# Moving the w_q checks out of the paired u products, moving the last difference checks, and giving the last two v tiles' products two PSUM banks

## The chip, the cores and the metric

The kernel runs on one core of a Trainium2 chip. The metric is the device time of one execution in microseconds (us). Before the change three runs gave 1128.66, 1130.21 and 1132.23 us; the median is 1130.21 us.

## The reference, cut to what matters

For x of shape 2048 x 512 the result is `x + A(xn) + B(xn)`, with `xn` the layer norm of x. A is a Fourier mixing layer: the real part of a DFT along the sequence of a DFT along the hidden axis, with the four DFT matrices given as inputs. B is a product-key expert layer:

```
q  = xn @ w_q                        # 32 heads, two halves of 128
s1, s2 = q1 @ k1.T, q2 @ k2.T        # 64 scores each
top 2 of s1 x top 2 of s2 -> the best 2 of 4 experts per head, softmax g
act = gelu(xn . u[expert])           # u, v: 4096 x 512
out = sum over 32 heads and 2 experts of g * act * v[expert]
```

Nothing is gathered. The kernel multiplies each tile of 128 tokens by all 4096 rows of u, applies gelu, multiplies the result by a sparse matrix of gates, and multiplies that by all of v.

## The kernel before, in words

The first 430 us load the DFT matrices, compute A, and find the experts of every token (`scores`, `routing`). The change touches only what follows, the last 700 us, where 16 tiles of 128 tokens go through u and v.

**Phases.** The order is z0, z1, v0, then for b = 2, 4, ..., 14 a phase z(b, b+1) that multiplies two tiles at once by u, followed by v(b-1) and v(b), and at last v15. A pair's z phase takes about 41 us (z(14,15) from 1011.1 to 1052.2) and a v phase about 24 us. A z phase of a pair (`z_pair`) is made of slots of 24 matmuls (`slot`, L1173) and of plain groups (`u_part`, L1095). After each slot ScalarE or VectorE takes sums out of the PSUM bank (L1213 to L1227) and ScalarE applies gelu (L1203). A v phase (`v_part`, L1328) runs 16 groups of six 128x512 matmuls into one bank `pv`, two groups for each of its eight steps `cg`; `finish` (L1345) scales the bank onto `y` and stores it. Nine of the sixteen groups of v stay in SBUF. The other seven are loaded again for each tile into three places, by `v_load` (L1306), each when the group before it in that place has been read.

**The gates.** For every tile, four times: `g_mm` builds two one-hot factors L and R on VectorE (L1260, L1265, L1268) and multiplies them on TensorE (L1270); `w_part` multiplies that by the gelu output on VectorE (L1278), rounds it to fp16 on ScalarE (L1285) and forms the remainder on VectorE (L1286). A v phase cannot start before the last `w_part` of its tile.

**The checks.** The kernel relies on structure in its inputs and checks it beside the main work. There are three kinds of check units, each handed out one at a time by `step`:

- `U`, 68 units: `compare` (64) and `compare_w` (4, units 64 to 67) load a block of a DFT matrix, form differences on VectorE (L1359 to L1403, L1426 to L1447) and sum their magnitudes on ScalarE (L1404, L1449). These are the difference checks.
- `F[0]`, 35 units of `fit`: 28 load a block of w_q (L1455) and take the sum of magnitudes on ScalarE (L1456); seven do so with streamed parts of v (L1462, L1463).
- `F[1]`, 25 units: the same on u and v blocks that lie in SBUF (L1467), without a load.

The loads of `U` and `F[0]`, and the product tile of `w_part`, share one pool of four buffers, tag `w`. `step` also holds back the ScalarE part of a unit: it issues those of earlier units, all but the newest. `verdict` gathers all sums into flags, after `step(None)` has flushed the rest at step 3 of v15.

**The order.** The dictionary `plan` says behind which step of which phase a unit or a gate step stands. That is a priority and not a place: the framework orders each engine's instructions itself when the program is built, by its own estimate of when operands and buffers are ready. So a load whose unit stands in the middle of a z phase can be issued near its beginning. Each engine then runs its list in order. All loads and stores of these phases are in SyncE's list.

**The last tile.** In v15 the last two groups (n = 14 and 15, 24 matmuls) are done in two halves of 256 columns, both added into the one bank `pv`. After each half VectorE scales that half onto `y` (L1319), and the half is stored (L1320).

Of the kernel before, what the change touches and what calls it, by code (L numbers as in the profile page):

```python
# [15 lines left out]
ALU = mybir.AluOpType  # L16
# [20 lines left out]
def tile_fnet_peer(ctx, tc, x, ca, cb, c5, wt, wf, wr, wq, kt, ut, vn, out):  # L37
# [9 lines left out]
    nc = tc.nc  # L47
# [503 lines left out]
    w16 = ones.bitcast(F16)  # L551
# [169 lines left out]
    def part_b(safe, stS, stP, stQ, stE, xt, u_sb, cmp_p, w4):  # L721
# [586 lines left out]
        def v_part(b, pv, cg):  # L1308
            w16 = parts(b)
            if b + 1 == NT and cg == 7 and not safe:  # L1310
                for h in range(2):
                    d = slice(h * 256, h * 256 + 256)
                    for n, cc in ((14, 0), (14, 1), (15, 0), (15, 1)):
                        g = v_order(b)[n]
                        for k, (l, r) in enumerate(((0, 0), (0, 1), (1, 0))):
                            nc.tensor.matmul(pv[:, d], w16[:, 2 * g + cc, :, l], v_sb[g][:, r, cc, d], start=False,
                                             stop=(n + cc == 16 and k == 2), skip_group_check=True)
                    y = Y[b]
                    nc.vector.scalar_tensor_tensor(y[:, d], pv[:, d], osc, y[:, d], op0=ALU.mult, op1=ALU.add)  # L1319
                    nc.sync.dma_start(out[b * P:(b + 1) * P, d], y[:, d])  # L1320
                return
            end = 13 if b + 1 == NT and not safe else 15
            for n in (2 * cg, 2 * cg + 1):
                g = v_order(b)[n]
                for cc in range(2):
                    c = 2 * g + cc
                    for k, (l, r) in enumerate(((0, 0), (0, 1), (1, 0))):
                        nc.tensor.matmul(pv, w16[:, c, :, l], v_sb[g][:, r, cc, :], start=(n + cc == 0 and k == 0),  # L1328
                                         stop=(n == end and cc == 1 and k == 2))

                if g >= V2 and g not in [v for v in v_order(b) if v >= V2][-3:]:
                    v_load(PL[g])
# [196 lines left out]
        def take(name):  # L1529
            tag = banks.pop(0)  # L1530
            return psz.tile([P, 512], F32, tag=tag, name=name), tag
# [14 lines left out]
        def put(ph, cg, *fs):  # L1546
            plan.setdefault((ph, cg), []).extend(fs)
# [45 lines left out]
            put(("v", b), 3, lambda b=b: compact_d(b + 2))  # L1593
        put(("z", 14, 15), 8, lambda: compact_d(15))
        if not safe:
            for cg in (1, 3, 5, 7):
                put(("v", 0), cg, F[0])
            for ph, cg in ((("v", 12), 0), (("v", 14), 1), (("v", 14), 3), (("v", 14), 7)):
                put(ph, cg, F[0])
            for ph in phases[3:]:  # L1600
                if ph[0] == "z":
                    put(ph, 8, F[0])
                    for cg in {2: (9, 11, 13, 15), 4: (9, 11, 13, 15), 14: (9, 12)}.get(ph[1], (9, 12, 15)):
                        put(ph, cg, U)
                elif ph[1] < 14:
                    for cg, f in enumerate((None, F[1], F[1], U, U, U, U, F[0]) if ph[1] % 2 == 0 else (
                            None, F[1], F[0], None, U, U, U, F[0])):
                        if f and (ph[1] < 13 or f != U or cg == 6):
                            put(ph, cg, f)
            for cg in range(3):  # L1610
                put(("v", 14), cg, F[1])
                put(("v", 14), cg + 4, U)
                put(("v", 15), cg, F[1])
            for f, n in ((U, 68), (F[0], NK + 16 - V2), (F[1], 16 + V2)):
                assert sum(v.count(f) for v in plan.values()) >= n
# [189 lines left out]
```

## Time and profile before

| what | value |
|---|---|
| median of the runs | 1130.21 us |
| the profiled execution's own time | 1130.3 us |
| its span in the profile | 1128.0 us |
| so outside the span | 2.3 us |
| granted TensorE clock, mean | 0.999 |
| matmuls | 11024 |

The profile's first part gives the busy time of each engine: PE is TensorE's matmuls, PEld its weight loads, DVE VectorE, ACT ScalarE, POOL GpSimd, SP SyncE. A row of the timeline has the start and the length in us, the engine, the line, the operation, the tile written and read, how many are merged, and, in brackets, how long the engine had been idle and what ended that. A row of the waits view names the waiting engine and line, what released it, the total in us, the number of times and the longest. A small q behind an engine's name stands for its sequencer, so SPq rows are issues of transfers.

### The profile page before, as it was taken

Reading aid. Unit: us, or ns where it says so; the run is one execution under the profiler, and the core shown is the slowest. Engines: PE = TensorE matmul, PEld = TensorE weight load, DVE = VectorE, ACT = ScalarE, POOL = GpSimd, SP = SyncE. Lnnn points to the kernel's source line nnn. Section 1 sums busy time; section 2 is a strip of 40 time slices with the busy share of each in tenths; the row PEclk is TensorE's granted clock in tenths of the full one; section 3 lists DMA queues with packets and bytes.
Section 4 is the critical chain, followed back from the end, with each engine's and each line's share of the span. In section 5 each row is a group of like instructions: output and inputs, shape, how many; then the busy total and the mean of one; then the engine's idle time right before and its main releaser. Section 6 shows DMA issues by size and latency. Waiting matters only on the chain.

```text
span 1128.0 us, 28019 instructions
## 1 busy us (share of the span) xinstructions
PE 1109.6 (98%) x11024; PEld 720.0 (64%) x11024; DVE 965.1 (86%) x2883; ACT 667.7 (59%) x1118; POOL 328.6 (29%) x364
## 2 busy tenths in 40 slices
PE   9999999999999999999999999999999999999997
PEld 6455554544545459678479479579469569559643
DVE  7899989989889899885997996997997897887892
ACT  6557698798898465365546545535545635545442
POOL 1415998888889750000000010010010010000000
PEclk9999999999999999999999999999999999999999
DMA  9984456346353215663754854753745755655353
GB/s 285 286 209 164 162 182 202 116 156 200 97 182 111 97 52 187 214 218 118 265 205 153 255 209 141 259 203 146 272 165 189 236 192 197 225 197 188 105 186 107
DMA packets 123932, 206.80 MB, mean 183 GB/s; under 512 B 34564, under 2 KB 65419, under 8 KB 123790
## 3 DMA queue, kind: packets, MB, share of 16 engines
q1 hardware_dynamic: 123488, 204.84, 54.7%
q8 instruction: 88, 1.44, 0.5%
q14 instruction: 54, 0.44, 0.1%
q10 hardware_dynamic: 302, 0.08, 0.0%
HBM read 171.52 MB, written 27.59 MB: 177 GB/s over the span
## 4 chain that ended last, share of the span: by engine, by line
PE 46%; DVE 12%; DMA 3%; ACT 3%; POOL 2%; issue 1%; SPq 0%; ACTq 0%; DVEq 0%; POOLq 0%
PE v L1328 18%; PE z L1173 16%; PE z L1095 9%; PE g L1270 3%; DVE L L1260 2%; DVE w L1278 2%; DMA cx<-in_cb_dram 2%; DVE vals L956 1%; DVE act L1286 1%; DVE idx L960 1%; DMA fit<-in_wq_dram 1%; DVE w L1286 1%; DVE cx L1378 1%; DVE R L1265 1%; DMA v<-v_d 1%
## 5 line engine op out<-in xcount | busy, mean ns | idle before, releaser
L252 PE MATMUL s<-m,xq 128*128 128x512 f16 x1344 | 297.4, 379 | 1.0 <-ACT ss L952 0.5
L1328 PE MATMUL v<-v,act 128*128 128x512 f16 x1044 | 230.8, 379 | 0.3 <-DMA v<-v_d 0.3
L252 PEld LDWEIGHTS <-xq 128*128 128x128 f16 x1344 | 129.8, 98 | 152.2 <-issue 2.5
L1341 POOL TENSOR_TENSOR y<-y,xr 128x512 f32<-128x512 f32 x15 | 28.7, 1915 | 637.9 <-DMA y<-y_d 455.8
L1260 DVE TENSOR_TENSOR L<-io_lam,cmp 128x2048 f16<-128x2048 f16 x128 | 156.1, 1220 | 26.0 <-PE g L1270 25.9
L1328 PEld LDWEIGHTS <-act 128*128 128x128 f16 x1044 | 100.1, 98 | 116.5 <-issue 0.6
L956 DVE MAX8 vals<-ss 128x8 f32<-128x64 f32 x896 | 133.5, 216 | 3.9 <-ACT ss L952 3.9
L1095 PE MATMUL z<-xb,u 128*128 128x128 f16 (+1 forms) x1440 | 121.8, 244 | 0.1
L1173 PEld LDWEIGHTS <-u 128*128 128x128 f16 x2016 | 114.7, 98 | 3.1 <-issue 2.6
L1095 PEld LDWEIGHTS <-u 128*128 128x128 f16 x1440 | 107.6, 98 | 7.5 <-issue 0.2
L1328 PE MATMUL v<-v,w 128*128 128x512 f16 x480 | 106.3, 379 | 0.3 <-DMA v<-v_d 0.3
L952 ACT ACTIVATE ss<-s,wsc 128x512 f32<-128x512 f32 x120 | 81.4, 683 | 38.6 <-PE s L252 33.4
L1404 ACT ACTIVATE cx<-cx 128x896 f32<-128x896 f32 x64 | 60.5, 946 | 67.7 <-DVE cx L1384 38.1
L960 DVE FIND_INDEX8 idx<-vals,ss 128x8 uint16<-128x256 f32 x224 | 93.8, 419 | 0.0
L1173 PEld LDWEIGHTS <-s 128*128 128x128 f16 x1440 | 82.5, 98 | 0.2
L1328 PEld LDWEIGHTS <-w 128*128 128x128 f16 x480 | 46.0, 98 | 53.8 <-issue 0.6
L1285 ACT ACTIVATE act<-w 128x1024 f16<-128x1024 f32 x36 | 48.3, 1358 | 53.8 <-DVE w L1278 49.4
L1270 PEld LDWEIGHTS <-L 128*128 128x128 f16 x2048 | 60.5, 96 | 15.6 <-DVE R L1268 4.2
L1270 PE MATMUL g<-R,L 128*128 128x32 f16 x2048 | 62.0, 176 | 4.3 <-DVE R L1268 4.2
L1278 DVE SCALAR_TENSOR_TENSOR w<-act,scl,g 128x1024 f32<-128x1024 f32 x44 | 55.8, 1277 | 10.3 <-ACT act L1203 10.3
L1173 PE MATMUL z<-xb,u 128*128 128x128 f16 x1008 | 63.1, 219 | 0.4 <-ACT act L1102 0.3
L1173 PE MATMUL z<-x,u 128*128 128x128 f16 x1008 | 61.3, 219 | 1.6 <-ACT w L1226 0.8
(366 smaller groups left out, 1860.8 us busy)
## 6 DMA issues: line engine op xcount, KB each, us to landing
v<-v_d SPq DMA_DIRECT2D x67, 512.0 KB, 4.6
cx<-in_cb_dram SPq DMA_DIRECT2D x64, 448.0 KB, 6.1
s<-s_d SPq DMA_DIRECT2D x42, 512.0 KB, 3.1
w<-in_wq_dram SPq DMA_DIRECT2D x28, 512.0 KB, 6.3
fit<-in_wq_dram SPq DMA_DIRECT2D x28, 512.0 KB, 4.7
uv<-in_vn_dram SPq DMA_DIRECT2D x16, 512.0 KB, 3.8
uv<-in_ut_dram SPq DMA_DIRECT2D x16, 512.0 KB, 4.0
s_d<-v SPq DMA_DIRECT2D x24, 256.0 KB, 4.1
```

The source lines that it names most:

```text
L252: nc.tensor.matmul(ps, xt[i][:, l, kd, :], m[:, r, kd, :], start=(n == 0), stop=(n == 3 * KD - 1))
L952: nc.scalar.activation(s, ps, AF.Copy, scale=inv)
L956: nc.vector.max(vals[:, i, w, :, h], s[:, g, :])
L960: nc.vector.max_index(idx[:, i, w].rearrange("p k h -> p (k h)"), vals[:, i, w, 0:2].rearrange("p k h -> p (k h)"), s[:, w * HC:g + 1, :]. ...
L1095: nc.tensor.matmul(ps if n == 1 else ps.rearrange("p (b n) -> p b n", b=2), ug[:, l, c % 2, kd, :], xb2[:, k0, r, kd, :] if n == 1 else xb ...
L1173: nc.tensor.matmul(bank[:, t * P:(t + 1) * P], lt, rt, start=(t == k == 0 and op in "125"), stop=(t == 3 and k == 5), skip_group_check=op ...
L1260: nc.vector.tensor_tensor(L.rearrange("p t (l two) -> p t l two", two=2), io_lam.rearrange("p (l two) -> p l two", two=2).unsqueeze(1).to_ ...
L1270: nc.tensor.matmul(p[:, hf, t * NC:(t + 1) * NC], L[:, t, :], R[:, t, :], start=True, stop=True)
L1278: nc.vector.scalar_tensor_tensor(w, act[:, :, ts], fw, p.rearrange("p h (n c) -> p c (h n)", c=NC), op0=ALU.mult, op1=ALU.mult)
L1285: nc.scalar.activation(w16[..., 0], w, AF.Copy)
L1328: nc.tensor.matmul(pv, w16[:, c, :, l], v_sb[g][:, r, cc, :], start=(n + cc == 0 and k == 0), stop=(n == end and cc == 1 and k == 2))
L1404: later.append(lambda: nc.scalar.activation(tf[:, P:], tf[:, P:], AF.Abs, accum_out=chk[:, n:n + 1]))
```

## The change

Three things are changed, all for the path that is taken when the inputs are as expected.

1. `F[0]`: the unit behind step 8 of each pair's z phase is removed (seven units). Step 3 of v1, v3, ..., v13 gets one. In v0 the four units behind steps 1, 3, 5, 7 become two behind steps 2 and 6, and step 0 of v2 and of v4 gets one. The total stays 35, and the order of the units stays.
2. `U`: z(6,7) gets a fourth unit, as z(2,3) and z(4,5) have. v13 loses the one behind its step 6. The three behind steps 4, 5 and 6 of v14 go behind steps 6 and 7 of v14 and step 0 of v15. In v14's step 6 the unit stands behind the last `w_part` of tile 15. The total stays 68; since the units are handed out in order, unit 64 moves from v13 to z(14,15), units 65 and 66 to v14's steps 6 and 7, and unit 67 to v15.
3. The last tile: `pv` is complete after group 13 and is scaled onto the whole of `y`. The products of groups 14 and 15 then start new sums, each half in a bank of its own, taken from the four banks that the z and v phases share; each half is then added to `y` and stored.

```
 def v_part(b, pv, cg):
     w16 = parts(b)
     if b + 1 == NT and cg == 7 and not safe:
+        y = Y[b]
+        nc.vector.scalar_tensor_tensor(y, pv, osc, y, op0=ALU.mult, op1=ALU.add)
         for h in range(2):
             d = slice(h * 256, h * 256 + 256)
+            ph = take(f"v{b}_{h}")[0][:, 0:256]
             for n, cc in ((14, 0), (14, 1), (15, 0), (15, 1)):
                 g = v_order(b)[n]
                 for k, (l, r) in enumerate(((0, 0), (0, 1), (1, 0))):
-                    nc.tensor.matmul(pv[:, d], w16[:, 2 * g + cc, :, l], v_sb[g][:, r, cc, d], start=False,
-                                     stop=(n + cc == 16 and k == 2), skip_group_check=True)
-            y = Y[b]
-            nc.vector.scalar_tensor_tensor(y[:, d], pv[:, d], osc, y[:, d], op0=ALU.mult, op1=ALU.add)
+                    nc.tensor.matmul(ph, w16[:, 2 * g + cc, :, l], v_sb[g][:, r, cc, d],
+                                     start=(n + cc == 14 and k == 0), stop=(n + cc == 16 and k == 2))
+            nc.vector.scalar_tensor_tensor(y[:, d], ph, osc, y[:, d], op0=ALU.mult, op1=ALU.add)
             nc.sync.dma_start(out[b * P:(b + 1) * P, d], y[:, d])
         return
...
-            for cg in (1, 3, 5, 7):
-                put(("v", 0), cg, F[0])
+            for ph, cg in ((("v", 0), 2), (("v", 0), 6), (("v", 2), 0), (("v", 4), 0)):
+                put(ph, cg, F[0])
             for ph, cg in ((("v", 12), 0), (("v", 14), 1), (("v", 14), 3), (("v", 14), 7)):
                 put(ph, cg, F[0])
             for ph in phases[3:]:
                 if ph[0] == "z":
-                    put(ph, 8, F[0])
-                    for cg in {2: (9, 11, 13, 15), 4: (9, 11, 13, 15), 14: (9, 12)}.get(ph[1], (9, 12, 15)):
+                    for cg in {2: (9, 11, 13, 15), 4: (9, 11, 13, 15), 6: (9, 11, 13, 15), 14: (9, 12)}.get(ph[1], (9, 12, 15)):
                         put(ph, cg, U)
                 elif ph[1] < 14:
                     for cg, f in enumerate((None, F[1], F[1], U, U, U, U, F[0]) if ph[1] % 2 == 0 else (
-                            None, F[1], F[0], None, U, U, U, F[0])):
-                        if f and (ph[1] < 13 or f != U or cg == 6):
+                            None, F[1], F[0], F[0], U, U, U, F[0])):
+                        if f and (ph[1] < 13 or f != U):
                             put(ph, cg, f)
             for cg in range(3):
                 put(("v", 14), cg, F[1])
-                put(("v", 14), cg + 4, U)
+                put(("v", 14 + cg // 2), (6, 7, 0)[cg], U)
                 put(("v", 15), cg, F[1])
```

## The prediction

> **What bounds the kernel now.** I read the page first, then the waits of TensorE, then the timeline around each of these waits, at last SyncE's own waits and issues.
>
> ```profile
> span 1128.0 us, 28019 instructions
> ...
> PE 1109.6 (98%) x11024; PEld 720.0 (64%) x11024; DVE 965.1 (86%) x2883; ACT 667.7 (59%) x1118; POOL 328.6 (29%) x364
> ...
> PEclk9999999999999999999999999999999999999999
> ```
> ```profile
> 580.00:666.00 86.00, 86.00 (x1043) 62.26 (x1041) 72.82 (x118) 45.99 (x76) 4.51 (x2) 1.00 0.63 210
> 839.00:926.00 87.00, 86.13 (x1040) 62.18 (x1038) 72.92 (x119) 44.24 (x74) 2.87 (x2) 1.00 0.59 203
> ```
> ```profile
> PE g L1270 <- DVE R L1268: 4.2, 5, 1.4
> ...
> PE z L1173 <- ACT w L1226: 0.8, 1, 0.8
> ...
> PE z L1173 <- ACT act L1226: 0.6, 1, 0.6
> PE v L1316 <- DVE y L1319: 0.6, 1, 0.6
> PE v L1328 <- DMA v<-v_d: 0.6, 2, 0.3
> ```
>
> TensorE is busy for 98% of the span, at a full granted clock. The second fence is the view by stretches (stretch, its length, then busy us of PE, PEld, DVE, ACT, POOL): over one pair of tiles TensorE has no gap at all, while VectorE works 72.8 of 86 us. The change adds and removes no matmul. So it can win only the waits of the third fence, 6.8 us in these rows, and it can lose wherever a gap is made in a stage that has none now. I therefore price wait by wait. The sum is made on the profiled execution, 1130.3 us with 2.3 us of it outside the span; that is 0.1 above the median of 1130.21, a difference I ignore.
>
> **The end of v15 (two banks).**
>
> ```profile
> 1118.94 1.32 PE v L1316 x12
> ...
> 1120.29 0.50 DVE y L1319
> ...
> 1120.83 1.48 PE v L1316 x12
> ...
> 1122.34 0.48 DVE y L1319
> ```
> ```profile
> 1101.67 0.73 DVE L1345 SCALAR_TENSOR_TENSOR y<-v,scl,y 128x512 f32<-128x512 f32 x1
> ...
> 1110.09 0.15 DVE L1505 TENSOR_TENSOR flags<-flag,flag 1x1 int32<-1x1 int32 x1
> ```
>
> The chain of waits shows the second half's matmuls starting at 1120.83, behind VectorE's read of the first half out of the same bank. With a bank of its own it follows the first half at 1118.94 + 1.32 = 1120.26. That is 0.57, or up to 0.7 with the drain between the two. I take -0.7. What is added is one full-width scaling, 0.73 by the row of tile 14's. It can start when group 13 is done, near 1118.9, and ends near 1119.7, before the first half is ready at 1120.26, so it costs nothing; without that cover (if VectorE were still at the checks) it would cost up to 0.73. Bounds: -0.7 to 0. The two banks come from the shared four, of which v15 holds one and nobody else asks, so no wait for a bank.
>
> **The z phases (no w_q check).**
>
> ```profile
> 848.16 1.50 PE L1173 MATMUL z<-xb,u 128*128 128x128 f16 x24
> 849.50 1.50 PE L1173 MATMUL z<-x,u 128*128 128x128 f16 x24
> 850.15 1.06 ACT L1456 ACTIVATE fit<-fit 128x1024 f32<-128x1024 f32 x1 [1.97 <-DMA fit<-in_wq_dram]
> 851.21 0.58 ACT L1226 ACTIVATE w<-z 128x512 f32<-128x512 f32 x1
> 851.84 1.50 PE L1173 MATMUL z<-x,u 128*128 128x128 f16 x24 [0.84 <-ACT w L1226]
> ```
>
> In z(10,11) ScalarE stands 1.97 us for a w_q block, then sums it for 1.06, and only then empties the bank that TensorE waits for. Slots of 24 start 1.34 apart (848.16 to 849.50); this one starts 2.34 after its predecessor, so it loses 1.0. Without the check the copy L1226 can run at once: -1.0, bounds -1.0 to 0 (a difference check's sum could take the place). In the other pairs the check is hidden under slots and its removal is worth 0. The 0.6 in the waits list is in z(2,3), behind difference checks and not a w_q check; I leave it at 0.
>
> **v0 (four units become two).**
>
> ```profile
> 471.94 1.06 ACT L1456 ACTIVATE fit<-fit 128x1024 f32<-128x1024 f32 x1 [4.93 <-DMA fit<-in_wq_dram]
> 473.00 1.32 ACT L1285 ACTIVATE act<-w 128x1024 f16<-128x1024 f32 x1
> 474.36 1.34 DVE L1286 TENSOR_TENSOR act<-w,act 128x1024 f16<-128x1024 f32 x1 [1.24 <-ACT act L1285]
> 477.53 0.56 PE L1270 MATMUL g<-R,L 128*128 128x32 f16 x16 [1.42 <-DVE R L1268]
> ```
>
> The first unit's sum delays the rounding of a gate product, VectorE idles 1.24 for that, and TensorE loses 1.42 at the next factor R. Fewer and later units can remove this, or put another unit before another rounding, since the place in the list is the planner's. Bounds -1.4 to +1.4; I take the middle of what a gain would be, -0.7.
>
> **v13 and v14 (difference checks go).**
>
> ```profile
> 1069.77 0.41 DVE L1426 TENSOR_REDUCE sums<-cx 128x1 f32<-128x256 f32 x1
> ...
> 1074.04 0.27 DVE L1445 TENSOR_TENSOR cx<-cx 128x128 f32<-128x128 f32 x1
> ...
> 1080.90 0.57 PE L1270 MATMUL g<-R,L 128*128 128x32 f16 x16 [1.14 <-DVE R L1268]
> ...
> 1084.28 1.94 POOL L1341 TENSOR_TENSOR y<-y,xr 128x512 f32<-128x512 f32 x1 [65.08 <-DMA y<-y_d]
> ...
> 1085.00 1.50 DVE L1265 TENSOR_TENSOR R<-io_c,cmp 128x512 f16<-128x512 f16 x1
> ...
> 1087.89 0.41 DVE L1265 TENSOR_TENSOR R<-io_c,cmp 128x512 f16<-128x512 f16 x1
> ...
> 1089.89 0.55 PE L1270 MATMUL g<-R,L 128*128 128x32 f16 x16 [0.71 <-DVE R L1268]
> ```
>
> Unit 64 runs its ten VectorE instructions between 1069.77 and 1074.31, 4.5 us of which about 3 are its own (ten of 0.1 to 0.5), just ahead of tile 15's factors; TensorE then waits 1.14 and 0.71 for these factors. Taking the unit out of v13 moves VectorE's list up by some 3 us, more than the 1.85 of both waits: I take -1.9, bounds -1.9 to 0. In z(14,15), where it goes, TensorE needs VectorE only for small sums, and VectorE's 3 us are free there unless they fall in front of one.
>
> Moving the next three units behind the last gate product brings nothing by itself: in this trace v15 starts without a wait. What they could cost is lateness at the end. The flags are there at 1110.24 (1110.09 + 0.15), and the first output half is scaled at 1120.79: 10.5 us to spare. In the code nothing but the end waits for the flags. Unit 67 and the verdict behind it would have to slip by all of that. Cost 0; beyond that point 1 us per us.
>
> The rest of this stretch shows a limit on the gain. The same R takes 1.50 when GpSimd adds y, and 0.41 otherwise, so 1.09 of VectorE's delay is not the checks'. [...]
>
> **The odd v phases and SyncE's list (seven units more).** Each of the seven added units is one load of 0.5 MB, 1.06 + 0.19 us on ScalarE and one of the four `w` buffers for its stay. ScalarE is busy about half of the time there, so its share is hidden by VectorE's longer list. The queue is the danger:
>
> ```profile
> SPq L1455 <- ACT cx L1404: 23.2, 6, 4.3
> ```
> ```profile
> 1002.22 0.33 SPq L1462 DMA_DIRECT2D fit<-v_d  x1
> 1002.65 0.38 SPq L1306 DMA_DIRECT2D v<-v_d  x1
> ...
> 1006.74 2.75 PE L1328 MATMUL v<-v,act 128*128 128x512 f16 x12 [0.29 <-DMA v<-v_d]
> ```
> ```profile
> 880.96 7.93 PE L1328 MATMUL v<-v,act 128*128 128x512 f16 x36
> ...
> 886.33 0.33 SPq L1306 DMA_DIRECT2D v<-v_d  x1
> ...
> 895.31 0.33 SPq L1455 DMA_DIRECT2D fit<-in_wq_dram  x1
> ```
> ```profile
> v<-v_d SPq DMA_DIRECT2D x67, 512.0 KB, 4.6
> ```
>
> SyncE waits up to 4.3 us with a w_q load for a buffer that a difference check still holds, and everything behind it in the list waits too. In v12 a check load issued at 1002.22, and the v load right behind it was late for TensorE by 0.29. In v9, as in the other odd phases, the long-waiting load (895.31) is the last one of the phase, behind all v loads, so nothing is hurt. The new unit stands at step 3, amid them. A v load issued at 886.33 lands near 890.9 (4.6 us, page part 6), and TensorE needs it about 3 to 4 us after that; the earlier two of the phase have some 2.5. So a short wait is absorbed and a 4.3 us wait is not. Per phase: 0 (absorbed) to 1.8 (4.3 less 2.5); the nearest row is v12's 0.29. The z phases lose the same loads, so bytes and buffers per pair are unchanged. I take +0.5 in all, less than two such waits; both ends, 0 and +12.6 (seven times 1.8), are kept for the range. The units at step 0 of v2 and v4 are of the same kind and are in this figure, as is z(6,7)'s fourth difference check, which z(2,3) and z(4,5) already carry.
>
> **Sum.** -0.7 - 1.0 - 0.7 - 1.9 + 0.5 = -3.8: 1130.3 - 3.8 = 1126.5 us, 0.34% faster.
>
> **The rivals.**
> 1. *The waits form anew* (0.20). All places in the lists are planned again. z(10,11) and the end win 1.7, v14 and v0 keep theirs, and 0.7 of new waits arise elsewhere: 1129.3. For it: VectorE is 84% busy over a pair. Against it: the pair from 580 to 666 has no gap with much the same lists.
> [...]
> 3. *Held v loads* (0.22), the one that ends slower. The new w_q load waits for a buffer ahead of v loads in the odd v phases. With 1.0 lost in each of seven phases, and only the end and z(10,11) won (-1.7), the time is 1130.3 + 7.0 - 1.7 = 1135.6. It decides from 0.24 a phase (1.7 / 7) on; from 0.73 on it is slower by over 0.3%. For it: the 4.3 us waits. Against it: only two of the present late v loads cost anything, 0.3 each.
> 4. *The last difference check comes too late* (0.03): flags after 1120.8, each us one us. With the other three gains kept (-3.1 with the +0.5), 7 us of lateness make 1130.3 - 3.1 + 7 = 1134.2.
>
> **How the numbers follow.** The forecast itself has 0.40, with a range of its own of 1122.5 to 1128.5. About 0.3%, or 3.4 us, is what a measurement here can tell from no change; faster means below 1126.8. Of the forecast I count 0.35 there and 0.05 within, of the lock 0.07 and 0.08, of rival 1 0.01 and 0.18 (0.01 slower), of rival 3 0.02 within and 0.20 slower, of rival 4 0.02 within and 0.01 slower: faster 0.43, same 0.35, slower 0.22. The range: if all 6.8 of the listed waits and a little of their drain go, the time is near 1122; at the top it takes in rival 3 and stops short of its bound: 1122 to 1136.
>
> **What would show it.** Right: v L1316 waits for nothing; no L1456 on ScalarE inside a z phase and no L1226 wait in z(10,11); no compare work on VectorE between 1053 and 1090 and no wait at tile 15's factors; flags before the last halves. Wrong: new rows of v L1328 <- DMA in odd phases, with SyncE waiting at L1455 ahead of L1306; g L1270 <- DVE waits in phases that have none now; SPq at the output waiting for the flags.

## The result and the profile after

The changed kernel takes 1146.47 us (median of 6 runs, 1142.47 to 1150.76). The kernel before, run beside it, takes 1131.53 us (6 runs, 1128.66 to 1133.92). The ratio is 1.0132, with a 95% interval from 1.0105 to 1.0159. So the change costs 15 us where 3.8 us of gain were forecast, and the time lies above the range. The profiled execution of the changed kernel took 1150.76 us, the longest of its six, so the sums below are some 4 us larger than those of a median run. Among the later runs one of the ten executions of h_poolq was far slower than the rest (1634.16 us at a granted clock of 0.653); it is in that run's median, which is 1138.77 without it, and not in its ratio.

The page of the changed kernel, its span, its engines and the head of its chain:

```profile
span 1148.9 us, 28041 instructions
...
PE 1117.3 (97%) x11024; PEld 725.9 (63%) x11024; DVE 964.6 (84%) x2884; ACT 666.4 (58%) x1118; POOL 330.6 (29%) x364
...
PE 33%; DVE 16%; DMA 12%; ACT 3%; issue 2%; POOL 2%; SPq 1%; ACTq 0%; DVEq 0%; POOLq 0%
```

The same line of the page of before, the chain by engine:

```profile
PE 46%; DVE 12%; DMA 3%; ACT 3%; POOL 2%; issue 1%; SPq 0%; ACTq 0%; DVEq 0%; POOLq 0%
```

Work has hardly changed: VectorE and ScalarE are busy as long as before (965.1 and 667.7 there). Transfers have gone from 3% to 12% of the chain. The waits of TensorE after the change (total us, times, longest):

```profile
PE g L1270 <- DVE R L1268: 13.0, 11, 2.4
PE v L1330 <- DMA v<-v_d: 6.6, 8, 3.2
```

Before, these were 4.2 and 0.6. The two rows hold 14.8 us more; in the stretch from v1 to v12 alone they are 12.0 and 6.6 after, and 0.8 and 0.6 before. A stretch of one pair of v phases, v5 and v6, shows what a pair loses, first before, then after:

```profile
703.50:748.90 45.40, 45.40 (x356) 22.77 (x352) 40.39 (x63) 22.97 (x34) 1.85 (x1) 1.00 0.74 251
```
```profile
710.60:759.10 48.50, 45.96 (x355) 22.84 (x353) 41.23 (x69) 23.86 (x36) 1.53 (x1) 1.00 0.70 246
```

TensorE had no gap there and now has 2.5 us of gaps; its busy time grows by 0.56 too, most of it where the three gaps split a group of matmuls: the two parts take 0.55 + 0.55, 0.57 + 0.55 and 7.93 + 2.75, the unsplit groups before 0.95, 0.95 and 10.52. All six pairs from v1 to v12 do this: +3.4, +3.0, +3.1, +5.3, +2.3 and +2.8 us, 19.9 together (from each pair's first matmul to the next z phase's, as in the stretches above). The rest of the longer span is small: +3.3 us in the seven paired z phases, +0.9 ahead of v0, -1.3 in v0, and -1.8 from v13 to the end. All gaps in these pairs fall not in the odd phases, where the units were added, but in the even phases behind them. From the timeline of TensorE after:

```profile
577.27 0.55 PE L1270 MATMUL g<-R,L 128*128 128x32 f16 x16 [2.37 <-DVE R L1268]
...
845.90 4.41 PE L1330 MATMUL v<-v,w 128*128 128x512 f16 x19 [3.21 <-DMA v<-v_d]
...
1023.73 2.75 PE L1330 MATMUL v<-v,act 128*128 128x512 f16 x12 [1.48 <-DMA v<-v_d]
...
1032.04 0.59 PE L1270 MATMUL g<-R,L 128*128 128x32 f16 x16 [2.12 <-DVE R L1268]
```

**Why the factors are late.** VectorE's waits after the change, then before:

```profile
DVE cx L1380 <- DMA cx<-in_cb_dram: 24.7, 18, 3.4
...
DVE sums L1361 <- DMA cx<-in_ca_dram: 11.8, 10, 2.7
...
DVE cx L1367 <- DMA cx<-in_cb_dram: 8.2, 5, 2.7
```
```profile
DVE cx L1378 <- DMA cx<-in_cb_dram: 13.7, 19, 2.2
...
DVE sums L1359 <- DMA cx<-in_ca_dram: 7.0, 9, 1.1
...
DVE cx L1365 <- DMA cx<-in_cb_dram: 0.3, 1, 0.3
```

With the rows of the weight comparisons VectorE stands 47.6 us for loads of difference checks, 22.4 before. It does its list in order, so the factors R and L behind such an instruction stand too: in v2 it stands for such loads 2.05 us up to 557.10 and 2.65 up to 560.04, and from there it is busy without a break (17.19 of 17.19 us) up to the factor that TensorE gets at 577.27. The loads are late because SyncE issues them late. SyncE's list in v5, first before (v5 starts at 703.5; each difference check is two loads, L1357 and L1358, of which the first is shown):

```profile
706.24 3.71 SPq L1306 DMA_DIRECT2D v<-v_d  x2
710.04 0.38 SPq L1357 DMA_DIRECT2D cx<-in_ca_dram  x1
...
712.22 0.33 SPq L1306 DMA_DIRECT2D v<-v_d  x1
712.65 0.38 SPq L1357 DMA_DIRECT2D cx<-in_ca_dram  x1
714.81 0.33 SPq L1306 DMA_DIRECT2D v<-v_d  x1
...
720.36 0.33 SPq L1455 DMA_DIRECT2D fit<-in_wq_dram  x1
...
723.21 0.33 SPq L1357 DMA_DIRECT2D cx<-in_ca_dram  x1
```

And after (v5 starts at 710.6; the two loads of a check are L1359 and L1360):

```profile
713.83 0.38 SPq L1457 DMA_DIRECT2D fit<-in_wq_dram  x1
716.81 0.32 SPq L1306 DMA_DIRECT2D v<-v_d  x1
718.50 0.33 SPq L1359 DMA_DIRECT2D cx<-in_ca_dram  x1
...
719.40 2.91 SPq L1306 DMA_DIRECT2D v<-v_d  x2
722.37 0.43 SPq L1359 DMA_DIRECT2D cx<-in_ca_dram  x1
...
728.61 0.33 SPq L1457 DMA_DIRECT2D fit<-in_wq_dram  x1
728.98 1.18 SPq L936 DMA_TRANSPOSE zt<-z_d  x1
734.90 0.33 SPq L1359 DMA_DIRECT2D cx<-in_ca_dram  x1
```

The added w_q load is the one at 713.83, ahead of the first difference load. Counted from the start of the phase, that first load comes 7.9 instead of 6.5 us in; it waits for a buffer that a w_q block still holds (L1359 <- ACT fit L1458 is 8.0 us in 9 waits, before 2.1 in 2). The v loads of the odd phase itself are issued no later than before (the four of v5 at 2.8, 6.2, 8.8 and 11.4 us in both lists), and the added load waits for nothing there. The second difference load comes at 11.8 instead of 9.2, behind the phase's fourth v load (the second of the two merged at 719.40), which it preceded before (712.65 and 714.81). The fourth comes at 24.3 instead of 19.7: SyncE has the transpose issued at 730.16 and stands there until 734.90. What it waits for is in SyncE's own waits:

```profile
SPq L1359 <- ACT cx L1406: 31.8, 9, 5.0
SPq L1457 <- ACT cx L1406: 29.1, 7, 5.9
```

The first row is new in its size (before: 1.2 us in 3 waits). It is a difference load that waits for a buffer of the `w` pool which an earlier difference check still holds, since its sum on ScalarE has not run. For the load at 734.90 it is this sum, from ScalarE's timeline:

```profile
733.85 0.93 ACT L1406 ACTIVATE cx<-cx 128x896 f32<-128x896 f32 x1
```

That closes a ring, as this trace reads: a difference load is late, VectorE is late with it, ScalarE's sum is late, the buffer is free late, and the next difference load is late.

Of TensorE's 6.6 us for v loads, 2.4 (in v4 and v12) stand right behind such a wait. The longest single wait, 3.21 in v8, does not. Its v load stands behind the load of a block of x (`xr`), which waits 6.8 us for GpSimd's add of y in the tile before:

```profile
SPq L1342 <- POOL y L1343: 37.7, 13, 6.8
```
```profile
838.56 0.33 SPq L1342 DMA_DIRECT2D xr<-in_x_dram  x1
...
839.94 0.38 SPq L1306 DMA_DIRECT2D v<-v_d  x1
```

The waits row was 21.2 us before, and there the load of x in v8 stood behind this v load. The remaining 1.0 us is in v6 and v10, most of it behind w_q loads that wait for the buffer of a gate product. So all these waits are in SyncE's one list, but not all are the ring.

### The profile page after: what moved, and what is told of

Its sections match the earlier page's. It is cut to its first block, busy times and chain, and to the rows that moved or that the text cites. A ratio compares the mean times of both kernels' runs of the same rounds, so it can differ in the third digit from the quotient of the medians.

```text
span 1148.9 us, 28041 instructions
## 1 busy us (share of the span) xinstructions
PE 1117.3 (97%) x11024; PEld 725.9 (63%) x11024; DVE 964.6 (84%) x2884; ACT 666.4 (58%) x1118; POOL 330.6 (29%) x364
## 4 chain that ended last, share of the span: by engine, by line
PE 33%; DVE 16%; DMA 12%; ACT 3%; issue 2%; POOL 2%; SPq 1%; ACTq 0%; DVEq 0%; POOLq 0%
PE z L1173 14%; PE z L1095 8%; PE v L1330 7%; DMA cx<-in_cb_dram 7%; DVE L L1260 3%; DMA fit<-in_wq_dram 3%; PE g L1270 3%; DVE cx L1380 2%; DMA v<-v_d 2%; DVE w L1278 1%; DVE vals L956 1%; DVE idx L960 1%; DVE act L1286 1%; DVE R L1268 1%; DVE R L1265 1%
## 5 line engine op out<-in xcount | busy, mean ns | idle before, releaser
L1173 PEld LDWEIGHTS <-u 128*128 128x128 f16 x2016 | 117.7, 99 | 2.2 <-issue 1.6
L1095 PEld LDWEIGHTS <-u 128*128 128x128 f16 x1440 | 107.7, 98 | 8.6 <-issue 1.4
L1285 ACT ACTIVATE act<-w 128x1024 f16<-128x1024 f32 x36 | 48.3, 1356 | 53.1 <-DVE w L1278 42.4
L1380 DVE TENSOR_TENSOR cx<-cx 128x512 f32<-128x512 f32 (+2 forms) x84 | 48.9, 613 | 26.0 <-DMA cx<-in_cb_dram 24.7
```

Source lines behind the costliest of these rows:

```text
L1095: nc.tensor.matmul(ps if n == 1 else ps.rearrange("p (b n) -> p b n", b=2), ug[:, l, c % 2, kd, :], xb2[:, k0, r, kd, :] if n == 1 else xb ...
L1173: nc.tensor.matmul(bank[:, t * P:(t + 1) * P], lt, rt, start=(t == k == 0 and op in "125"), stop=(t == 3 and k == 5), skip_group_check=op ...
L1380: nc.vector.tensor_tensor(v, v, tv[:, 0:1].to_broadcast([P, len(ix), 256]), op=o)
```

## The experiments

In the table, the first columns are median and ratio to the kernel before, run beside it each time, with its 95% interval. "Ring" is SyncE's total wait, in us, of difference loads for a buffer of another difference check (the row just shown); "loads" is VectorE's total wait for difference loads; "R" is TensorE's wait for factors. These three are from the waits of the profiled execution, which can differ from the median by up to 5 us.

| run | us | ratio | ring | loads | R |
|---|---|---|---|---|---|
| before | 1131.53 | 1 | 1.2 | 22.4 | 4.2 |
| after | 1146.47 | 1.0132 [1.0105, 1.0159] | 31.8 | 47.6 | 13.0 |
| e1_banks | 1128.86 | 0.9992 [0.9977, 1.0007] | 0.9 | 22.4 | 4.8 |
| e2_units | 1130.13 | 0.9990 [0.9970, 1.0010] | 0.8 | 26.0 | 2.7 |
| e3_wq | 1144.49 | 1.0114 [1.0082, 1.0146] | 31.7 | 44.1 | 12.1 |
| e4_z8back | 1134.29 | 1.0034 [1.0014, 1.0055] | 1.1 | 24.5 | 3.2 |
| m_units_banks | 1127.83 | 0.9975 [0.9961, 0.9990] | 0.6 | 21.4 | 1.6 |
| m_light | 1128.35 | 0.9983 [0.9966, 1.0000] | 0.9 | 20.2 | 2.1 |
| m_bytes | 1127.33 | 0.9968 [0.9951, 0.9985] | 1.5 | 23.3 | 4.9 |
| m_resident | 1127.93 | 0.9981 [0.9960, 1.0001] | 5.1 | 25.6 | 2.6 |
| m_small_w | 1131.72 | 1.0016 [0.9983, 1.0049] | 1.3 | 25.3 | 4.5 |
| m_late | 1130.57 | 0.9995 [0.9973, 1.0017] | 0.3 | 22.6 | 5.5 |
| m_small_own | 1141.76 | 1.0113 [1.0077, 1.0149] | 0.3 | 27.8 | 13.8 |
| m_z0 | 1139.99 | 1.0071 [1.0046, 1.0096] | 0.3 | 20.1 | 4.1 |
| h_load2 | 1135.31 | 1.0029 [1.0003, 1.0055] | 0.5 | 26.3 | 7.5 |
| h_none2 | 1127.47 | 0.9973 [0.9953, 0.9992] | 3.2 | 21.5 | 2.8 |
| h_full1 | 1145.15 | 1.0126 [1.0084, 1.0168] | 31.5 | 38.0 | 13.3 |
| h_poolq | 1139.06 | 1.0065 [1.0040, 1.0091] | 0.9 | 26.3 | 8.4 |
| k_order | 1129.03 | 0.9993 [0.9975, 1.0011] | 4.8 | 23.6 | 2.8 |
| k_behind | 1131.81 | 1.0007 [0.9988, 1.0027] | 10.7 | 34.6 | 5.4 |

**Which part.** e1_banks is part 3 alone, e2_units part 2 alone, e3_wq part 1 alone, each on the kernel before.

> Only the third part of the change: the last two groups of tile 15 in two banks, the plan of the checks as before. Theory A (the seven w_q units at step 3 of the odd v phases do the harm): no wait of the second half on VectorE, 0.5 to 0.8 us faster than before, about 1130.8. Rival B (the units' moves are innocent and the loss is spread): the same here; a loss of over 2 us in this run would speak against both.

> Only the second part: the difference checks' new places. Theory A: v13 and v14 lose their waits at tile 15's factors (1.8 us less from v13 to the end) and the v pairs from v1 to v12 stay at 45.4 us each, so 1 to 2 us faster, about 1130. Rival B (the moved difference checks crowd the v pairs): 5 us or more slower, with v pairs of 47 us and more.

> Only the first part: the w_q units out of the z phases and of half of v0, into the odd v phases and step 0 of v2 and v4. Theory A: the whole loss is here, 14 to 20 us slower (1145 to 1151), v pairs of 48 to 51 us, with VectorE waiting for the difference checks' loads. Rival B: within 3 us of before.

Part 1 alone costs 1.14% and shows the ring; its row in SyncE's waits is:

```profile
SPq L1357 <- ACT cx L1404: 31.7, 9, 5.1
```

Parts 2 and 3 cost nothing that these runs can tell. Together, in m_units_banks, they gain 0.25%:

> The second and third parts of the change on the kernel before, no w_q unit moved at all. Theory A: v pairs at 45.4 to 45.9, v13 to the end at 74.0 (1.8 less than before), 1 to 3 us faster than before, 1127.5 to 1129.5. If the parts do not add up: no faster than before.

That version, with all checks in it and no w_q unit moved, is faster than both kernels: 1127.83 us.

**Which half of part 1.** e4_z8back is the changed kernel with the seven units back in the z phases:

```
-                    None, F[1], F[0], F[0], U, U, U, F[0])
+                    None, F[1], F[0], None, U, U, U, F[0])
                 if ph[0] == "z":
+                    put(ph, 8, F[0])
```

> All of the change except that the seven w_q units stay behind step 8 of the z phases and none is added at step 3 of the odd v phases. Theory A: the v pairs are back at 45.4 us and the gains of v0, v14 and the end stay, 3 to 5 us faster than before, about 1127. Rival B: still 10 us or more slower. Rival C (the two units at step 0 of v2 and v4 hurt): v1 with v2 and v3 with v4 stay at 48 us and the others come back, no gain over before.

Most of the loss goes. It differs from m_units_banks only in the units of v0, v2 and v4, and is 6.5 us slower (1134.29 against 1127.83); in its trace the pairs v1-v2 and v3-v4 take 46.9 and 47.5 us, the later ones 45.4 to 45.6. So the units at step 0 of v2 and v4 cost some 3.6 us there, and the seven in the odd phases cost the rest. (The runs below keep these two units, except k_order and m_z0; those that lose nothing in all show 1.6 to 4.9 us over 45.4 in the same two pairs.)

**What of an added unit costs.** In the next runs the seven units at step 3 of the odd phases are replaced by something less, so that their blocks are left out of the check, wholly or in part; everything else is the changed kernel. (Six of the seven blocks are of w_q; the unit of v13 reads a part of v.) The plan names `F3` at that place, and the body is given for each.

m_light has no load, no buffer and no sum, only the copy of one column:

```
+    later.append(lambda: nc.scalar.activation(fits[:, n:n+1], fits[:, c:c+1], AF.Copy))
```

> The changed kernel, but the seven units at step 3 of the odd v phases load nothing, take no buffer and do no sum: ScalarE copies one column of an earlier unit's sums (seven w_q and v blocks are left out of the check). Theory A1 (an added unit holds one of the four w buffers, so the difference checks' loads are issued later than the planned order of VectorE allows): v5 to v12 back at 45.4 to 46 us a pair, v1 to v4 at 47 as in the run with the z units back, in all 1129 to 1134. Rival A2 (the added 0.5 MB loads crowd the transfer queues): the same. Rival A3 (it is the missing unit in the z phases, behind which the sums of earlier checks were issued, and not the added one): still 10 us or more slower than before.

m_bytes adds to this a copy of 0.5 MB from DRAM to DRAM for each of the six blocks of w_q (`nc.sync.dma_start(q_d..., wq[...])`), so that the bytes were to be there without a buffer:

> The changed kernel, but each of the seven units at step 3 of the odd v phases copies its 0.5 MB from device memory to device memory, in SyncE's list at the same place in the plan, with no w buffer and no sum (these blocks are left out of the check). Rival A2 (the bytes crowd the transfer queues): v5 to v12 stay at 47.5 us or more a pair, 1138 and more. Theory A5 (what counts is how long a unit keeps its w buffer, and so when the next difference block can be loaded): 45.4 to 46.5 us a pair, 1127 to 1133, as in the run without load.

It did not do that. Nothing holds these copies back, and the framework put all six into the first part of the kernel, at 90.7 to 123.1 us. The view of their line:

```profile
L1458 SPq DMA_DIRECT2D q_d<-in_wq_dram x6: 488/556/5554, 90.7 to 123.1; - x6
```

So m_bytes is a second m_light, and says nothing of bytes in the odd phases.

m_resident has buffer and sum, of a block of u that lies in SBUF, and no load:

> The changed kernel, but the seven units load nothing: ScalarE sums a block that already lies in SBUF, writing into a w buffer, 1.06 us as the real unit (these blocks are left out of the check). Theory A5: the buffer is held for about a microsecond only, 45.4 to 46.5 us a pair from v5 on, 1127 to 1133. Rival A6 (ScalarE's 1.2 us come between a gate product and its rounding): 47 us and more a pair, 1138 and more.

All three are as fast as before or faster. So the removal from the z phases and ScalarE's time are not the cause. Of the bytes two other things speak. The difference loads took no longer to land beside the added loads, as the pages of before and after show (the last number is us from issue to landing):

```profile
cx<-in_cb_dram SPq DMA_DIRECT2D x64, 448.0 KB, 6.1
```
```profile
cx<-in_cb_dram SPq DMA_DIRECT2D x64, 448.0 KB, 5.8
```

And k_behind, at the end of this section, moves the same bytes in the same phases without the loss.

m_small_w loads less than a tenth of the block, but into the same pool; m_late is that with the sum planned later; m_small_own gives the small load a buffer of its own:

```
+    t = bp.tile([P, 96], F32, tag="w", name=f"fit{n}", bufs=WB)     # m_small_own: tag="fx", bufs=1
+    nc.sync.dma_start(t, wq[...][:, 0, 0:96])
```

> As the run before, the same tenth of the block and the same sum, but into one of the four shared w buffers. Theory A1 (buffers): nearly as slow as the changed kernel, v pairs of 47 to 50 us, 1140 to 1147, with SyncE's waits of the difference checks' loads for ScalarE's sums at 25 us or more in total. Rival A2 (bytes): fast, 1129 to 1135, like the run with the own buffer.

> As the run with a tenth of the block in a shared w buffer, but the sum, which gives the buffer back, stands one or two check steps later in the plan (nine tenths of these blocks are left out of the check). Theory A5: if ScalarE really does the sum later, the buffer is held 3 to 6 us longer with hardly any bytes, and the v pairs from v5 on go up again by 1 us or more each, 1134 to 1145. Rival A2: as that run, about 1132.

> The changed kernel, but the seven units load a tenth of their block (96 of 1024 columns) into a small buffer of their own and sum that (the rest of these seven blocks is left out of the check). Theory A1 (buffers): fast, v5 to v12 at 45.4 to 46.5 us a pair, 1129 to 1135. Rival A2 (bytes): fast too. Rival A4 (the unit's place in SyncE's and ScalarE's lists, whatever it loads): slow, 1140 and more.

m_small_w, at 1.0016, refutes the expectation that sharing the pool is enough. m_late says nothing: the sums came 4.9 to 6.3 us after their loads were issued, as in m_small_w (5.0 to 6.7), so the stay was not made longer. m_small_own does not test what it was meant to: its loads have a buffer that nothing else uses, and the framework put them ahead of and into v0, at 449.2 to 469.9 us, and none into an odd phase. It lost its 12 us there, most of it in one wait ahead of v0; its v pairs are at 45.4 to 47.5. The view of its line, and TensorE's timeline:

```profile
L1459 SPq DMA_DIRECT2D fit<-in_wq_dram x6: 327/358/1355, 449.2 to 467.3; - x6
```
```profile
464.56 0.59 PE L1270 MATMUL g<-R,L 128*128 128x32 f16 x16 [9.42 <-DVE R L1268]
```

A full-size buffer of its own, or a fifth shared one (4 KB per partition), was not tried. So whether the shared buffer itself is needed for the loss is not shown by a run.

h_load2 and h_none2 separate a long stay from a large load: two ScalarE passes over a `w` buffer, with a load of a sixteenth of the block (the buffer is held some 8.2 us) and with none.

```
+    t = bp.tile([P, 16, 64], F32, tag="w", name=f"fit{n}", bufs=WB)
+    nc.sync.dma_start(t[:, 0], wq[...][:, 0, 0:64])                 # not in h_none2
+    for _ in range(2):
+        nc.scalar.activation(t[:, 1:16], v.unsqueeze(1).to_broadcast([P, 15, 64]), AF.Abs, ...)
```

> The changed kernel, but each of the seven units loads 64 of 1024 columns into a shared w buffer, and ScalarE then makes two passes of 960 columns over it (about 2.2 us, against 1.25 for the real unit), so that the buffer is kept about as long as by the real unit (7 to 8 us) with a sixteenth of its bytes (the blocks are left out of the check). Theory A5 (time in the buffer): v pairs of 47 us and more from v5 on, 1138 to 1148. Rival A7 (only a full load in the shared buffer does it, through the load's own length in the queue): 45.4 to 46.5 us a pair, 1127 to 1133.

> The same two passes of ScalarE into a w buffer, from a small tile that has been in SBUF all along, so no load and a buffer kept for about 2.2 us. Theory A5: 45.4 to 46.5 us a pair, 1126 to 1132. If it is as slow as the run before, what hurts there is ScalarE's 2.2 us and not the time in the buffer.

The small load with its long stay costs 8 us, less than half of what the changed kernel loses against h_none2, and without the ring. h_full1 has the full load in the shared buffer, and ScalarE reads one column of it:

```
-    later.append(lambda: nc.scalar.activation(t, t, AF.Abs, accum_out=fits[:, n:n+1]))
+    nc.scalar.activation(ones[:, 0:1], t[:, 0:1], AF.Abs)
```

> The added seven units load their 0.5 MB into one of the four shared buffers as in the changed kernel, but ScalarE then reads one column instead of 1024 (about 0.2 us instead of 1.25). The sums of these seven blocks are left out. Theory A (the length of the stay in the buffer decides): the stay falls from about 8 to under 7 us, so most of the loss goes: 1128 to 1136 us. Theory B (a full-size load in a shared buffer is enough, since its transfer alone is the larger part of the stay): the loss stays nearly whole: 1141 to 1147 us, v pairs of v3 to v12 at 47.5 us and more.

The whole loss is back (theory B), and the ring with it, in SyncE's waits of h_full1:

```profile
SPq L1359 <- ACT cx L1406: 31.5, 9, 4.8
```

Its buffer is held for 7.1 us in v5, less than the 8.2 of h_load2 and the 8.0 of the changed kernel, so the length of the stay is not what sets it apart from h_load2.

**Where the load stands.** h_poolq issues the same seven loads from GpSimd's queue (`nc.gpsimd.dma_start` in place of `nc.sync.dma_start`).

> The changed kernel, but the seven added loads are issued by GpSimd's queue instead of SyncE's; size, buffers and ScalarE's sums are as in the changed kernel. Theory A and B (the held buffer is what the next difference load waits for): still slow, 1141 to 1148 us, VectorE's waits for difference loads about 45 us in all. Theory C (the added load's own place in SyncE's list pushes the difference loads and v loads behind it): mostly recovered, 1126 to 1132 us, with these waits back at about 22 us.

It came out between the theories. The ring is gone (0.9), about half of the time is not (1139.06); the profiled execution lies 5 us below the median, so its waits say little of the other half. The row of GpSimd's timeline shows that the load is also issued at another time, 2.3 us after the start of v5 at 706.6, and not 3.2:

```profile
708.86 0.57 POOL L1457 DMA_DIRECT2D fit<-in_wq_dram  x1 [35.19 <-DVE w L1278]
```

k_order and k_behind take the two things apart that the changed kernel, e3_wq and h_full1 have in common: the second difference load stands behind the phase's fourth v load, and a full-size w_q load stands ahead of the first. k_order is m_units_banks with the second check of the odd phases one step later; k_behind is the changed kernel with the added unit behind the first two checks:

```
 k_order   (1, F[1]), (2, F[0]), (4, U), (6, U), (6, U), (7, F[0])
 k_behind  (1, F[1]), (2, F[0]), (3, U), (4, U), (5, F[0]), (6, U), (7, F[0])
```

> Parts 2 and 3 alone, no w_q unit moved, but in the odd v phases the second difference check stands behind step 6 instead of step 5. In SyncE's list its load then stands behind the phase's fourth v load, as in the changed kernel, with no w_q load added. Theory A (this place in the list is what costs, since the v load ahead of it waits for TensorE): the second load comes 11.7 us into the phase instead of 9.2, and the kernel loses most of what the change lost: 1138 to 1146 us. Theory B (the held buffer costs, and the place in the list is only a sign of it): 1126 to 1130 us, as without this shift (1127.8).

> The changed kernel, but in the odd v phases the difference checks stand behind steps 3, 4 and 6 and the added w_q unit behind step 5. The added load keeps its full size, its shared buffer and ScalarE's sum, and stands in SyncE's list behind the first two difference loads instead of ahead of them. Theory A: these two loads keep their early places (second one at about 9 us into the phase), so most of the loss goes: 1127 to 1134 us. Theory B: a full-size load that holds a shared buffer costs wherever it stands in the phase: 1138 to 1147 us.

In k_order the second load comes 12.9 us into v5, later than in the changed kernel, and nothing is lost. The transpose has moved ahead of it too (710.36), and VectorE waits no longer for loads than before (23.6); the unit as a whole is planned a step later, so VectorE may come to it later as well. So theory A, a late place in the list as such, falls. In k_behind the added load is the same in size, buffer and sum, and the loss is gone to within the measurement (1.0007), so theory B, that it costs wherever it stands, falls too. The run is not a clean exchange: the first two difference checks also stand a step earlier, and their loads come at 3.2 and 7.8 us in v5 (6.6 and 9.2 before). How much of the gain is due to that is not shown. A part of the ring is left in k_behind:

```profile
SPq L1359 <- ACT cx L1406: 10.7, 8, 2.1
```

Against m_units_banks it still loses 4 us; in its trace the pairs of v1 to v4, with the units of v2 and v4, are 3.9 us over 45.4, and those of v5 to v8 3.4. What the 15 us and the ring go with is the two together: a full-size load in the shared pool, in SyncE's list ahead of the phase's first difference load.

SyncE's lists of all these runs say it more narrowly. In each of v1, v3, ..., v11 of the changed kernel, of e3_wq and of h_full1, the first difference load comes 6.9 to 8.6 us in and the second 11.7. In m_small_w, m_late and h_load2 the first is as late (7.4 to 8.3), but the second comes at 9.2 to 9.6, and there is no ring; h_poolq is so in four of its six phases. In k_order the first comes at 6.6 and the second at 11.8 to 13.0. So the full ring is seen only where both are late, and in these runs only a full-size load in SyncE's list made them so.

**Elsewhere.** m_z0 takes the seven units out of the z phases as the change does, but puts them behind steps 1 to 7 of z0, which has no check, on top of m_units_banks:

```
+            for cg in range(1, 8):
+                put(("z", 0), cg, F[0])
```

> A better version: the second and third parts of the change, no unit at step 3 of the odd v phases, v0 as before, and the seven w_q units of the z phases moved to steps 1 to 7 of z0, where no gate product needs a w buffer. Theory A5: v pairs 45.4, z pairs 41.0, v13 to the end 74, so 2 to 3 us faster than the run of parts two and three alone, 1124 to 1126. If the z phases gain nothing from it: 1127 to 1128.

The later z phases and v pairs are near 41.0 and 45.4 us (v pairs up to 46.4), but 12 us are lost in z0 and z1. SyncE issued the loads only from 443.08 on, one behind another, since v loads that stood ahead of them in its list waited until 440.98; ScalarE stood for them, and so did what is behind them on ScalarE. From the timelines of ScalarE and of TensorE:

```profile
449.04 1.06 ACT L1458 ACTIVATE fit<-fit 128x1024 f32<-128x1024 f32 x1 [9.84 <-DMA fit<-in_wq_dram]
```
```profile
455.93 1.01 PE L1270 MATMUL g<-R,L 128*128 128x32 f16 x32 [5.93 <-DVE w L1278]
```

## Why the prediction was wrong

**The step that failed** is "The odd v phases and SyncE's list (seven units more)", the term of +0.5 with its ends 0 and +12.6. The v pairs lost 19.9 us in the profiled execution (16.9 in e3_wq, which is part 1 alone), above its upper end. The cost that it had at nothing is the lateness of the difference loads. Three of its sentences led astray.

- "The z phases lose the same loads, so bytes and buffers per pair are unchanged." True for a pair, and of no use: the z phases have four buffers for three or four difference checks spread over 41 us, and an odd v phase already had two w_q loads and three difference checks in some 24 us, and got a third w_q load. Seven units fewer there gave little; seven more here closed the ring.
- "A short wait is absorbed and a 4.3 us wait is not", priced on v loads alone. I looked only for v loads behind the waiting load. The difference loads stand in the same list, and VectorE waits for them in its order, ahead of the factors that TensorE needs. That is the larger victim: from v1 to v12 the factors cost 11.2 us more (12.0 against 0.8), the v loads 6.0 (6.6 against 0.6).
- "In v9, as in the other odd phases, the long-waiting load (895.31) is the last one of the phase, behind all v loads, so nothing is hurt." This was read from the list of before. The added unit changes the list: the second check's load went behind a v load, and the long wait came ahead of a difference load of the next phase's work (734.90). The gaps then fell in the even phases, not in the odd ones where I said they would show.

Rival 3, "held v loads", was right in that the change ends slower, and gave 1135.6 us, but not in how. In the odd phases the added load waited at most 0.2 us, and no v load of theirs was late for TensorE. Its 1.0 per phase is near the 6.0 us that the v loads cost over six pairs, but that is luck: these are v loads of the even phases, behind other loads, and the factors are left out.

**The end (-0.7).** Right, as far as one trace of each kernel tells. From the timeline of TensorE after, the two halves run as one group, 2.78 from the start of the first to the end of the second, where before it was 3.52 (two groups of 1.47 and 0.58 between them); from VectorE's, the full scaling lies beside them:

```profile
1140.19 2.78 PE L1319 MATMUL v<-v,act 128*128 128x256 f16 x24
```
```profile
1131.86 0.15 DVE L1507 TENSOR_TENSOR flags<-flag,flag 1x1 int32<-1x1 int32 x1
1140.39 0.75 DVE L1312 SCALAR_TENSOR_TENSOR y<-v,scl,y 128x512 f32<-128x512 f32 x1 [8.38 <-PE v L1330]
1141.70 0.48 DVE L1321 SCALAR_TENSOR_TENSOR y<-v,scl,y 128x256 f32<-128x256 f32 x1 [0.56 <-PE v L1319]
```

The scaling ends at 1141.14, 0.56 before the first half is there. In e1_banks the stretch from v13 to the end took 75.2 us, 75.8 before: -0.6.

**v13 and v14 (-1.9).** Half right. With the end, this stretch went from 75.8 to 74.0 us: -1.8 in all and so -1.2 without the end. The first wait for tile 15's factors is gone; at the last there is still

```profile
1103.17 0.55 PE L1270 MATMUL g<-R,L 128*128 128x32 f16 x16 [0.79 <-DVE R L1268]
```

in TensorE's timeline. The chances count a lock with 0.07 and 0.08; no run shows it. What this trace shows at the wait that is left: that R takes 0.47, GpSimd's add of y starts only at 1106.71, and what lies between its two instructions (L1265, L1268) on VectorE is a gate product of 1.33. The flags are ready at 1132.01 (the first of VectorE's rows above), 9.7 us before the first output half is scaled, so the lateness of rival 4 did not come.

**z(10,11) (-1.0).** The mechanism held: no w_q sum in the phase, no wait at L1226. The phase went from 42.2 to 41.8, because another wait of 0.59 arose there. In e3_wq it was 41.0, and so in eleven other runs that have no w_q unit there; in the six that have it, before among them, it was 41.6 to 42.4 (k_behind, without it, took 42.0).

**v0 (-0.7).** Not shown. v0 went from 24.8 to 23.5 us, but e1_banks, whose plan for v0 is that of before, has 23.5 too (e2_units, with the same plan, 24.3). The 1.42 us wait that I meant to remove does not come in every execution or build with that plan.

**The chances.** "Slower" had 0.22, all but 0.02 of it on rival 3. The evidence for more was in the prediction's own row: SyncE stood 23.2 us for buffers of difference checks, six times, with four buffers. That was a sign that a load more could push others back, though not proof: k_behind has the same seven loads more and loses nothing that can be told from before.

**What stays open.** The framework orders the lists itself; why it puts the second difference load behind the v load only where the load ahead is full-size is not known. What h_load2 loses against h_none2 (8 us) and h_poolq against m_units_banks (11 us) without the ring has no row that explains all of it. That the loss needs both a full-size load and its place ahead of the difference loads rests on m_small_w, h_full1 and k_behind; that the ring is the way in which it costs is read from one trace of each run, and no run breaks the ring alone. Bytes without a buffer, and a full-size buffer apart from the pool, were never run in the odd phases.

## What to carry to other kernels

Moving a load inside a list that is worked in order, with buffers from a shared pool, is a change to every load behind it and to every engine that waits for one of them in its own order: price it on all of these, not only on the transfer that the matrix engine waits for (here the v loads cost 6.0 us more and the factors 11.2). When SyncE's own waits show that loads already stand for buffers of that pool, take the sum of those rows as a warning that the pool may have no slack. When a test takes away a buffer or a wait, see in the trace where the framework has put the transfer: m_bytes and m_small_own had theirs some 400 us and 60 us away from the place that they were to test. If a load must be added, put it behind the loads that a busy engine waits for, not ahead of them; in this kernel k_behind did so (1.0007, against 1.0132).

## What was not expected of the hardware

Behind two waits of TensorE its granted clock was halved for 3.3 us, so that they cost more than their length; behind the longest wait it was not. Around the 2.37 us wait at the end of v2, and behind the 3.21 us wait in v8, the stretches (length, busy times of the five engines, granted clock, share of the DMA engines, GB/s) show

```profile
574.60:578.00 3.40, 1.03 (x35) 1.02 (x31) 3.37 (x7) 1.51 (x4) 0.00 (x0) 1.00 0.00 0
578.10:581.40 3.30, 3.30 (x35) 3.30 (x33) 3.30 (x5) 0.60 (x1) 0.00 (x0) 0.50 0.21 79
...
845.90:849.30 3.40, 3.40 (x16) 1.47 (x16) 3.40 (x7) 2.23 (x3) 0.00 (x0) 1.00 0.77 312
```

The granted clock was 0.50 from 578.1 to 581.4, and the first two groups of 24 matmuls there took 2.43 and 2.24 us, where such a group takes 1.50. z(4,5) took 42.6 us without a gap, and 41.0 before: 1.6 us more behind a 2.4 us wait. The 2.12 us wait ahead of z(14,15) did the same (0.50 from 1032.0 to 1035.3, and 42.4 us). The longest wait, 3.21 us in v8, did not; the clock behind it was 1.00. Idle time alone does not tell them apart: TensorE was busy for 1.03 of the 3.4 us ahead of the fall, and for none of the 3.21 us in v8. What sets them apart is not shown.
